# Shifted copies of two pairs of score tiles made by one VectorE instruction, in a planned attention and MLP kernel

## The chip, the core and the metric

The kernel runs on one core of one Trainium2 chip. The metric is the time on the device in microseconds, the median of the runs shown. Engines are named as in the profile: PE is TensorE (PEld its weight loads), DVE is VectorE, ACT is ScalarE, POOL is GpSimd, SP is SyncE, which issues the DMAs.

## What is computed

Two rounds of the same two layers, with the same weights each time, on x of 2048 tokens by 512 features in bfloat16:

```python
def _A_ref(x, wqkv, wo):            # H = 32 heads of Dh = 16
    q, k, v = ...                   # (x @ wqkv) split in heads
    p = _softmax(einsum("bhqd,bhkd->bhqk", q, k) * Dh ** -0.5)
    return heads_joined(einsum("bhqk,bhkd->bhqd", p, v)) @ wo

def _B_ref(x, w1, b1, w2, b2):      # F = 1376
    h = _gelu(einsum("bsd,df->bsf", _layernorm(x), w1) + b1)
    return einsum("bsf,fd->bsd", h, w2) + b2

x = x + _A_ref(_layernorm(x), A_wqkv, A_wo)
x = x + _B_ref(_layernorm(x), B_w1, B_b1, B_w2, B_b2)
# and both once more
```

The softmax over 2048 keys, for 2048 queries and 32 heads, twice, is the bulk: 268 million exponentials. In tiles of 128 keys by 512 queries that is 4096 tiles.

## The kernel before

**Tiles and stages.** The work is split in segments: a group of four heads (`hg`, eight of them) and a block of query tokens (512, in the last quarter of the second round 256, 128 and 128). For a segment, PE multiplies K and Q of one head and 128 keys into one bank of PSUM (`score`, L1512): a tile of 128 keys by 512 columns. Four heads sit in four row groups of PE. Then the tile is exponentiated in one of two ways.

- On ACT (L1497): PE fills two or three banks, banks 0 to 2 and 3 to 4 in turn, and one ACTIVATE makes `PT` of all of them (`flow_scores`).
- On DVE (`take_d`, `d_load`, `job_d`), for the key blocks in `DK` only: one TENSOR_SCALAR adds a constant to the scores and writes them as 16-bit integers into `dp` (L1598, one tile). The bits of such an integer, read as bfloat16, are nearly an exponential. Its error repeats along the exponent, so the kernel uses four copies, shifted by 0, 32, 64 and 96 and weighted in the values `vs`, to average it. Tiles go in batches of two (`DBATCH`), which fill one row of `dp` of 1024 elements. The first shift (L1629) makes row u+1 from row u. The second (L1634) makes rows v and v+1 from rows u and u+1.

PE then multiplies each copy with its values into one bank of sums (`try_pv`, L1705), four heads side by side in column groups. A tile of ACT's takes one such product, a tile of DVE's four. When a segment is done, DVE transposes the sums and divides (L1735, L1761, L1771), SP transposes the result by DMA (L1780), and the output product, the layer norm, both MLP products (L1846, L1907) and the GELU on ACT (L1898) follow, placed between the scores of later segments. Zero products (L1401, L1403, L1405) fill gaps of PE (`refill`).

**Buffers.** `dp` has 14 rows, handed out as pairs (even, odd) from a pool, oldest first; the pool's list grows as pairs are given up by other uses. In certain stages one more pair is lent by `OT`, a tensor of its own (`dpu`, `dpp` pick the right one). A pair goes back to the pool when the last product that reads it has been planned.

**What sets the order.** Nothing is ordered on the chip but by the engines' queues. A planner in Python (`Sched`) holds the tasks of all engines, each with a priority and an assumed duration; it picks the task that can start first, by the assumed times, and writes it into its engine's queue (`Prog.op`). A task counts as ready on DVE if its data is there within `LOOK` = 0.05 us of the time at which DVE comes free. What instructions wait for is worked out from reads and writes of named parts, such as ("dp", u, w). The string `Hint.ORDER` switches some of the planner's thresholds, one character for each four groups of scores; it moves work between ACT and DVE and reorders PE. The lines of the shifts, which the change wraps:

```python
yield Task("dve", prio(), [I(lambda e: e.tensor_scalar(out=self.dpu(u + 1)[:, 0:N], in0=self.dpu(u)[:, 0:N], ...)])   # L1629
self.d_ready(bt, 1, u + 1, u, range(n))
v = yield ("get", "dp", sg["i"])
yield Task("dve", prio(), [I(lambda e: e.tensor_scalar(out=self.dpp(v)[:, :, 0:N], in0=self.dpp(u)[:, :, 0:N], ...)])  # L1634
```

Their assumed durations are 0.150 + 0.2605e-3 N and 0.150 + 0.521e-3 N us, and DVE is taken to be free 0.08 us before an instruction ends.

Of the kernel before, what the change touches and what calls it, by code (L numbers as in the profile page):

```python
# [8 lines left out]
BF16 = mybir.dt.bfloat16  # L9
# [3 lines left out]
U16 = mybir.dt.uint16  # L13
ACTF = mybir.ActivationFunctionType
ALU = mybir.AluOpType
# [20 lines left out]
SHIFT = (0, 32, 64, 96)  # L36
# [5 lines left out]
class _Op:  # L42
    __slots__ = ("eng", "fn", "reads", "writes", "pos", "deps", "sig", "count", "waits", "dmaq", "t0", "t1", "spec", "spare")

    def __init__(self, eng, fn, reads, writes):
        self.eng = eng
        self.fn = fn
        self.reads = reads
        self.writes = writes
        self.pos = -1  # L50
        self.deps = []
        self.sig = False
        self.count = 0
        self.waits = []
        self.dmaq = None
        self.t0 = 0.0
        self.t1 = 0.0
# [196 lines left out]

class Task:

    __slots__ = ("eng", "ops", "prio", "cb", "seq")

    def __init__(self, eng, prio, ops):
        self.eng = eng  # L260
        self.prio = prio
        self.ops = ops
        self.cb = None
        self.seq = 0


def I(fn, reads=(), writes=(), dur=0.3, same_ok=(), lat=None):
    return (fn, tuple(reads), tuple(writes), tuple(same_ok), dur, lat)
# [9 lines left out]
class Sched:  # L278
# [45 lines left out]
    def _step(self, gen, prio, val):  # L324
        while True:
# [24 lines left out]
            if kind == "ready":  # L350
                r = self.P.ready(req[1], req[2], ()) - AHEAD
                if r <= self.now:
# [6 lines left out]
    def release(self, name, slot):  # L359
        p = self.pools[name]  # L360
        if slot in p.retired:
            key = p.retired.pop(slot)
            self.mark(key)
            return
        if p.waiters:
            _, _, cb = heapq.heappop(p.waiters)
            cb(slot)
        else:
            p.free.append(slot)

    def retire(self, name, slot, key):
        p = self.pools[name]
# [43 lines left out]
    def scores_due(self, f, lim):  # L416

        first = None
        for t in self.pend["pe"]:
            if t.prio == 0.0:  # L420
                r = self.task_ready(t)
                if r > lim and (first is None or r < first):
                    first = r
        if first is None or first - f > HOLD_REACH:
            return None
# [19 lines left out]
    def run(self):  # L445
        while True:
            pick = None
            for e in ENGINES:
                c = self.best(e)
                if c is not None and (pick is None or c[0] < pick[0]):  # L450
                    pick = c
            if self.timers and (pick is None or self.timers[0][0] <= pick[0]):
                t, _, cb = heapq.heappop(self.timers)
                self.now = max(self.now, t)
                cb()
                continue
            if pick is None:
                break
            t = pick[1]
            self.now = max(self.now, pick[0])  # L460
            if t.eng == "pe" and self.filler is not None:
                gap = pick[0] - self.P.drain
                if gap > FILL_GAP:
                    self.filler(gap)
            self.pend[t.eng].remove(t)
            for (fn, reads, writes, same_ok, dur, lat) in t.ops:
                self.P.op(t.eng, fn, reads, writes, same_ok, dur, lat)
            if t.cb is not None:
                t.cb()
            if t.eng == "dve" and self.after_dve is not None:  # L470
                self.after_dve()
        if self.live or self.kwait:
            raise RuntimeError("scheduler stuck: %d live, keys %s, pools %s" % (self.live, list(self.kwait)[:8], [(n, len(p.free), len(p.waiters)) for n, p in self.pools.items() if p.waiters]))


AHEAD = 0.3
HOLD_REACH = 1.0
HOLD_LEAD = 0.45
FILL_GAP = 0.2
# [13 lines left out]
DBATCH = 2  # L493
DFLY = 4
DBACK = 2.0
NDP = 14
# [19 lines left out]
NN2 = 2  # L516
NEED2 = 0
DOT = True


HELD = {(3, 0): (3, 1)}
# [2 lines left out]
class Hint:  # L524
    BASE = dict(D_IDLE=1.2, PV_LEAST=0.75, HOLD_LATE=0.4, PV_NEAR=0.7, LIN2=9, D_STEAL=0, POST=0)
    MODES = (dict(), dict(D_IDLE=0.8), dict(D_IDLE=1.7), dict(PV_LEAST=0.6), dict(PV_LEAST=0.9), dict(HOLD_LATE=0.2), dict(HOLD_LATE=0.6), dict(PV_NEAR=0.4), dict(LIN2=0.9), dict(D_STEAL=1.0), dict(POST=1), dict(POST=2))
    STEP = 4
    ORDER = '617843148821304222410024330100010322200010402005142300045935291731905421304450012300445404028299551400009505333207404304200030002302391015000030510104040320034300330030059090225910306350630422003320070322304130078057891b143300430303032703000430001459928b9001b338492908900532301308540020000009440105408040a010010a0211'

    def mode(self, k):  # L530
        self.__dict__.update(self.BASE)
# [2 lines left out]
    def at(self, step):  # L534
        self.mode(int(self.ORDER[step], 36) if step < len(self.ORDER) else 0)

# [5 lines left out]
class Builder:  # L542
# [45 lines left out]
    def alloc(self, es):  # L588
        nc = self.nc
        S, NT, NC, NFC = self.S, self.NT, self.NC, self.NFC  # L590
        t = lambda name, shape, dt: es.enter_context(nc.sbuf_tensor(name, shape, dt))
# [25 lines left out]
        self.qraw = t("qraw", [128, 2, 512], BF16)  # L617
        self.QT = t("QT", [128, 3, 512], BF16)
        self.PT = t("PT", [128, 23, 512], BF16)
        self.dp = t("dp", [128, NDP, 1024], U16)  # L620
        self.vs = t("vs", [128, 3, 3, len(DK), 68], BF16)
        self.OT = t("OT", [128, 8, 512], BF16)
        self.accT = t("accT", [128, 2, 512], F32)
        self.ob = t("ob", [128, 16, 8, 16], BF16)
        self.obl = t("obl", [128, 128], BF16)
# [81 lines left out]

    def otd(self, hg):

        return [("dp", NDP + (hg - 4) // 2, w) for w in (0, 1)] if DOT and hg >= 4 else []  # L710

    def dpu(self, u):

        return self.dp[:, u, :] if u < NDP else self.OT[:, 2 * (u - NDP) + 4:2 * (u - NDP) + 6, :].rearrange("p a n -> p (a n)").bitcast(U16)

    def dpp(self, u):

        return self.dp[:, u:u + 2, :] if u < NDP else self.OT[:, 4:8, :].rearrange("p a n -> p (a n)").bitcast(U16).rearrange("p (u n) -> p u n", u=2)

    def dres(self, s):  # L720

# [86 lines left out]
    def build_startup_late(self):  # L808
# [4 lines left out]
        def fills():  # L813
# [17 lines left out]
            S_.mark(("wld",))  # L831
            yield ("keys", [("retd", 1)] if DOT else [("oproj", 3, 0)])
            for hg in (6, 7):
# [744 lines left out]
    def d_solo(self):  # L1578
# [5 lines left out]
        if d is not None:  # L1584
            S_.submit(Task("pe", D_PRIO, self.score(d[0], d[1], d[2])), cb=lambda: self.d_load(d))

    def close_batch(self):
        bt = self.batch
        self.batch = None
        bt["closed"] = True  # L1590
        if bt["loaded"] == len(bt["tiles"]):
            self.S_.spawn(self.job_d(bt), 2.0)
# [30 lines left out]
    def job_d(self, bt):  # L1623

        S_ = self.S_
        u, n, sg = bt["unit"], len(bt["tiles"]), bt["tiles"][0][0]
        N = 512 * n
        prio = lambda: 0.15 if not self.left(sg) and sg is self.segs[self.acc_seg] else 0.5 if self.left(sg) < DURGE else 2.5
        yield Task("dve", prio(), [I(lambda e: e.tensor_scalar(out=self.dpu(u + 1)[:, 0:N], in0=self.dpu(u)[:, 0:N], scalar1=float(SHIFT[1]), scalar2=None, op0=ALU.add),  # L1629
                                     [("dp", u, w) for w in range(n)], [("dp", u + 1, w) for w in range(n)] + self.dres(u + 1), 0.150 + 0.2605e-3 * N, (), "fast")])  # L1630
        self.d_ready(bt, 1, u + 1, u, range(n))
        v = yield ("get", "dp", sg["i"])
        self.need2 -= 1
        yield Task("dve", prio(), [I(lambda e: e.tensor_scalar(out=self.dpp(v)[:, :, 0:N], in0=self.dpp(u)[:, :, 0:N], scalar1=float(SHIFT[2]), scalar2=None, op0=ALU.add),  # L1634
                                     [("dp", u + i, w) for i in (0, 1) for w in range(n)], [("dp", v + i, w) for i in (0, 1) for w in range(n)] + self.dres(v) + self.dres(v + 1), 0.150 + 0.521e-3 * N, (), "fast")])
        for i in (0, 1):
            self.d_ready(bt, 2 + i, v + i, v, range(n))
        self.flying -= 1
        self.use_done(("dp", u))
# [88 lines left out]
    def job_segend(self, sg):  # L1728
# [15 lines left out]
        if nparts == 2 and part == 0:  # L1744
            yield Task("dve", 1.2, [I(lambda e: e.tensor_copy(out=self.rowA[:, hg, :], in_=T[:, :, 17]), [RA], [("rowA", hg)], 0.25)])
            if L == 3:
                yield ("keys", [("oproj", 1, self.NC - 1)] + ([("retd", 0)] if DOT else []))
            yield Task("pool", 1.2, [I(lambda e: e.tensor_copy(out=M, in_=T[:, :, 0:16]), [RA], RO + [("sq", k, i) for k in (2, 3) for i in (0, 1)], 0.5), I(lambda e: e.tensor_copy(out=den, in_=T[:, :, 16]), [RA], [RD], 0.2)])
# [279 lines left out]
    def build(self):  # L2028
        S_ = self.S_
# [29 lines left out]
        S_.when([("qst", 1, tt) for tt in range(self.NT)], lambda: lend(1) if (1, 0) in HELD else None)  # L2059
        S_.when([("scl", 3, 1)] + [("qst", 3, tt) for tt in range(self.NT)], lambda: lend(3))  # L2060
        if DOT:
            S_.when([("ot", 1, 0, hg) for hg in range(8)], lambda: S_.release("dp", NDP))
            S_.when([("ot", 1, self.NC - 1, hg) for hg in range(8)], lambda: S_.retire("dp", NDP, ("retd", 0)))
            S_.when([("ot", 3, 0, hg) for hg in range(8)], lambda: S_.release("dp", NDP))
            S_.when([("ot", 3, len(self.units[3]) - 3, hg) for hg in range(8)], lambda: S_.retire("dp", NDP, ("retd", 1)))
        S_.when([("qt", 0)], lambda: S_.spawn(self.flow_scores(), 0.0))
        S_.filler = self.fill_pe
        S_.after_dve = self.d_solo
        self.P.spare = lambda: (tuple(range(6)) if self.wide and ("scores_done",) not in S_.done else ()) + ((MISCB,) if MISCB in S_.pools["mb"].free else ())
        for L in (1, 3):  # L2070
            for qc in range(len(self.units[L])):
# [58 lines left out]
```

## Time and profile before

| | |
|---|---|
| median of 3 runs | 1539.67 us (1539.26 to 1542.47) |
| the profiled execution | 1539.8 us, its span 1538.0 us |
| granted TensorE clock | 1.000 |
| exponentials on ACT (L1497) | 1260 instructions, busy 1427.3 us |
| tiles loaded by DVE (L1598) | 893 into dp and 78 into OT |
| first shifts (L1629) | 450 in dp and 39 in OT |
| second shifts (L1634) | 399, 51 and 39, by where they read and write |
| first exponential | at 21.2 us; last one ends at 1523.1 us |

The span runs from the first to the last instruction. In the rows of the groups stand line, engine, operation, output and input with their shapes (partitions by elements) and the count, then busy time in us and the mean duration in ns, then the engine's idle time before these instructions and what ended it. A row of the waits has who waited, for whom, the sum in us, how often, and the longest. A row of the timeline has the start and the length in us. Busy time counts overlapping instructions of one engine once; two instructions that follow each other overlap in the records, so the time that a queue spends on one is better read from start to start.

### The profile page before, as it was taken

The numbers are of one execution on the slowest core, as the hardware profiler recorded it, in microseconds if no ns is written. First come the engines' busy times: TensorE is split into PE (matmuls) and PEld (weight loads), VectorE is DVE, ScalarE is ACT, GpSimd is POOL, SyncE is SP. The second block draws the span as 40 slices with busy tenths as digits, with TensorE's granted clock in tenths as the row PEclk, the third lists the DMA queues.
The fourth block names the chain that finished last, engine by engine and source line by source line (L and its number), as shares of the span: only waits on it lengthen the run. The fifth ranks groups of instructions, "written<-read, shape, count | busy, mean of one in ns | idle before, by whom it ended". The sixth has DMA issues, their size and how long they took to land.

```text
span 1538.0 us, 41184 instructions
## 1 busy us (share of the span) xinstructions
PE 1485.6 (97%) x17604; PEld 489.9 (32%) x17604; DVE 1449.5 (94%) x2835; ACT 1508.2 (98%) x1350; POOL 333.9 (22%) x570
## 2 busy tenths in 40 slices
PE   8999999999999999999999999999999999999998
PEld 3222322222222222222222223222322222444565
DVE  8799999999999999999999899999999989999796
ACT  8999999999999999999999999999999999999997
POOL 3586422002120021202222228320002000020120
PEclk9999999999999999999999999999999999999999
DMA  6663102213321222213932333310011010210221
GB/s 166 116 150 87 35 26 40 57 26 79 84 42 52 49 56 75 62 33 99 149 52 67 60 77 72 58 26 21 22 33 39 11 29 24 45 41 25 72 68 31
DMA packets 212488, 90.56 MB, mean 59 GB/s; under 512 B 182251, under 2 KB 207184, under 8 KB 212304
## 3 DMA queue, kind: packets, MB, share of 16 engines
q1 hardware_dynamic: 212304, 87.92, 26.0%
q8 instruction: 138, 2.26, 0.6%
q14 instruction: 46, 0.38, 0.1%
HBM read 36.81 MB, written 19.48 MB: 37 GB/s over the span
## 4 chain that ended last, share of the span: by engine, by line
ACT 52%; PE 22%; DVE 21%; issue 2%; POOL 1%; SPq 1%; DMA 1%; POOLq 0%; DVEq 0%
ACT PT L1497 49%; DVE dp L1598 7%; PE ps L1512 7%; PE ps L1705 6%; DVE dp L1634 3%; PE ps L1907 3%; PE ps L1846 3%; DVE dp L1629 2%; ACT h L1898 2%; PE ps L992 2%; DVE st L909 1%; DVE accT L1735 1%; SPq L1780 1%; DMA OT<-ob 1%; DVE OT L1598 1%
## 5 line engine op out<-in xcount | busy, mean ns | idle before, releaser
L1497 ACT ACTIVATE PT<-ps 128x1536 bf16<-128x1536 f32 (+1 forms) x1260 | 1427.3, 1303 | 17.2 <-PE ps L1512 15.1
L1598 DVE TENSOR_SCALAR dp<-ps 128x512 uint16<-128x512 f32 x893 | 595.8, 681 | 33.4 <-PE ps L1512 30.8
L1512 PE MATMUL ps<-QT,KT 32*128 32x512 bf16 (+2 forms) x5120 | 599.5, 339 | 28.2 <-ACT PT L1497 10.9
L1705 PE MATMUL ps<-PT,V 128*17 128x512 bf16 (+2 forms) x3908 | 482.1, 338 | 0.0
L1705 PE MATMUL ps<-dp,vs 128*17 128x512 bf16 (+2 forms) x3318 | 433.5, 337 | 0.7 <-DVE dp L1634 0.4
L1512 PEld LDWEIGHTS ps<-QT,KT 32*128 32x128 bf16 x5120 | 172.5, 91 | 546.5 <-ACT PT L1497 307.2
L1634 DVE TENSOR_SCALAR dp<-dp 128x2048 uint16<-128x2048 uint16 (+1 forms) x399 | 277.2, 701 | 2.9 <-PE ps L1705 0.2
L1238 POOL TENSOR_SCALAR QT<-qraw,scl,qbias 128x512 bf16<-128x512 bf16 (+2 forms) x91 | 75.7, 832 | 766.0 <-PE ps L1512 753.6
L1705 PE MATMUL ps<-dp,V 128*17 128x512 bf16 (+2 forms) x1128 | 202.9, 337 | 1.5 <-DVE accT L1735 1.4
L1629 DVE TENSOR_SCALAR dp<-dp 128x1024 uint16<-128x1024 uint16 (+1 forms) x450 | 187.4, 428 | 2.3
L1405 PE MATMUL ps<-zw 128*32 128x448 bf16 (+25 forms) x1466 | 163.8, 324 | 0.4 <-DVE dp L1598 0.4
L1705 PEld LDWEIGHTS ps<-PT,V 128*17 128x17 bf16 x3908 | 124.7, 89 | 91.6 <-issue 75.0
L1705 PEld LDWEIGHTS ps<-dp,vs 128*17 128x17 bf16 x3318 | 117.9, 89 | 101.0 <-issue 74.8
L1403 PE MATMUL ps<-zw 32*128 32x444 bf16 (+2 forms) x387 | 120.5, 332 | 0.0
L1846 PE MATMUL ps<-yT,wf 128*128 128x512 bf16 (+5 forms) x440 | 103.7, 341 | 3.5 <-DVE dp L1629 1.5
L992 PE MATMUL ps<-wqkv,xnT 128*128 128x512 bf16 x336 | 92.1, 382 | 2.4 <-DVE dp L1005 0.9
L1401 PE MATMUL ps<-zw 128*128 128x448 bf16 (+16 forms) x371 | 90.1, 339 | 3.4 <-DVE onec L785 2.1
L1705 PE MATMUL ps<-OT,vs 128*17 128x512 bf16 (+2 forms) x318 | 78.0, 356 | 0.0
L1263 POOL TENSOR_SCALAR vs<-V 128x340 bf16<-128x340 bf16 (+2 forms) x72 | 62.7, 872 | 25.5 <-PE ps L1705 22.0
L1735 DVE STREAM_TRANSPOSE accT<-ps 128x512 f32<-128x512 f32 (+2 forms) x96 | 59.2, 617 | 7.0 <-PE ps L1705 7.0
L1405 PEld LDWEIGHTS ps<-zw 128*32 128x32 bf16 x1466 | 58.3, 95 | 19.6 <-DVE dp L1598 2.5
L1705 PEld LDWEIGHTS ps<-dp,V 128*17 128x17 bf16 x1128 | 50.8, 88 | 36.1 <-issue 18.3
(207 smaller groups left out, 1173.3 us busy)
## 6 DMA issues: line engine op xcount, KB each, us to landing
vs<-vs_scr SPq DMA_DIRECT2D x64, 255.0 KB, 2.7
wf<-in_B_w_dram SPq DMA_DIRECT2D x90, 128.0 KB, 2.5
q_scr<-qk SPq DMA_DIRECT2D x20, 256.0 KB, 2.0
k_scr<-qk SPq DMA_DIRECT2D x12, 256.0 KB, 2.0
out_dram<-xres SPq DMA_DIRECT2D x16, 128.0 KB, 1.7
vs_scr<-vs SPq DMA_DIRECT2D x8, 255.0 KB, 3.1
xres<-in_A_x_dram SPq DMA_DIRECT2D x7, 256.0 KB, 5.3
v_scr<-vst SPq DMA_DIRECT2D x12, 136.0 KB, 1.8
```

Of the source, the lines that this page charges most:

```text
L992: yield Task("pe", prio if c0 == 0 else min(prio, HINT.LIN2), [I(lambda e, c=c: e.matmul(self.ps[:, b, :], lhsT=xnT[:, c, :], rhs=self.wqk ...
L1238: yield Task(eng, 0.4, [I(lambda e: e.tensor_scalar(out=self.QT[:, q, 0:W], in0=src, scalar1=self.scl[:, k, hg:hg + 1], scalar2=self.qbias ...
L1401: fn = lambda e: e.matmul(self.ps[:, b, 0:w], lhsT=self.zw[:, 0:128], rhs=self.zw[:, 0:w], start=st, stop=st, skip_group_check=True)
L1403: fn = lambda e: e.matmul(self.ps[:, b, 0:w], lhsT=self.zw[32 * p:32 * p + 32, 0:128], rhs=self.zw[32 * p:32 * p + 32, 0:w], start=st, sto ...
L1405: fn = lambda e: e.matmul(self.ps[32 * p:32 * p + 32, b, 0:w], lhsT=self.zw[:, 0:32], rhs=self.zw[:, 0:w], start=st, stop=st, skip_group_c ...
L1497: S_.submit(Task("act", 1e-5 * gi, [I(lambda e, pt=pt, n=n, b0=b0: e.activation(out=self.PT[:, pt:pt + n, :], in_=self.ps[:, b0:b0 + n, :] ...
L1512: return [I(lambda e, kb=kb, i=i: e.matmul(self.ps[:, b, i * W:(i + 1) * W], lhsT=self.KT[32 * hp:32 * hp + 32, hg, kb * 128:(kb + 1) * 12 ...
L1598: self.S_.submit(Task("dve", 0.0, [I(lambda e: e.tensor_scalar(out=self.dpu(u)[:, w * 512:(w + 1) * 512], in0=self.ps[:, b, :], scalar1=BI ...
L1629: yield Task("dve", prio(), [I(lambda e: e.tensor_scalar(out=self.dpu(u + 1)[:, 0:N], in0=self.dpu(u)[:, 0:N], scalar1=float(SHIFT[1]), sc ...
L1634: yield Task("dve", prio(), [I(lambda e: e.tensor_scalar(out=self.dpp(v)[:, :, 0:N], in0=self.dpp(u)[:, :, 0:N], scalar1=float(SHIFT[2]), ...
L1705: ops.append((nth[j, sh] + 0.1 * i, I(lambda e, hp=hp, v=v, ap=ap[:, i * W:(i + 1) * W], first=first and i == 0, W=W: e.matmul(self.ps[32 ...
L1846: yield Task("pe", self.soft(pr if c0 == 0 else min(pr, HINT.LIN2)) if y0 == 0 else pr, [I(lambda e, c=c: e.matmul(self.ps[0:M, b, 0:W], l ...
```

## The change

A shift of a full batch (two tiles) carries a `mate`: its kind (1 or 2) and its rows. When the planner picks such a task, it looks for another of the same kind on DVE that is ready by then and whose rows lie in the same order, and emits one instruction for both, over two rows with the distance of the two batches as step. The joined instruction reads and writes what both did and waits for both; what follows either is released after it. It is planned 0.15 us shorter than both together.

So that two batches can be one access pattern, the pair of rows lent by `OT` moves behind the 14 rows of `dp` into one tensor (`bits`, 18 rows, of which the last four are `OT`; `LENT` is 16). The pool of pairs is sorted after each release, so that the lowest pair goes out first. And `Hint.ORDER` is a new string.

```diff
+            if name == "dp":
+                p.free.sort()
...
+            both = None
+            if t.mate is not None:
+                lim = max(pick[0], self.P.free["dve"]) + self.LOOK["dve"]
+                both = next((o for o in self.pend["dve"] if o.mate is not None and o.mate[0] == t.mate[0] and (o.mate[1] < t.mate[1]) == (o.mate[2] < t.mate[2]) and self.task_ready(o) <= lim), None)
+            if both is not None:
+                self.pend["dve"].remove(both)
+                (fn, reads, writes, same_ok, dur, lat), more = t.ops[0], both.ops[0]
+                x, y = sorted((t.mate[1:], both.mate[1:]))
+                self.P.op("dve", self.join(t.mate[0], x, y), reads + more[1], writes + more[2], same_ok, dur + more[4] - SHIFT_FIXED, lat)
+                for o in sorted((t, both), key=lambda o: o.mate[1:]):
+                    o.cb()
+            else:
...
+SHIFT_FIXED = 0.15
...
+LENT = NDP + 2
...
-        self.dp = t("dp", [128, NDP, 1024], U16)
+        self.bits = t("dp", [128, NDP + 4, 1024], U16)
+        self.dp = self.bits[:, 0:NDP, :]
...
-        self.OT = t("OT", [128, 8, 512], BF16)
+        self.OT = self.bits[:, NDP:NDP + 4, :].bitcast(BF16).rearrange("p u (a n) -> p (u a) n", n=512)
...
+    def both(self, a, b, o=None):
+
+        if o is not None:
+            return self.bits[:, a + o:b + o + 1:b - a, :]
+        return self.bits[:, :, :].rearrange("p (u a) n -> p u (a n)", a=2)[:, a // 2:b // 2 + 1:(b - a) // 2, :]
...
+    def d_join(self, kind, x, y):
+
+        if kind == 1:
+            return lambda e: e.tensor_scalar(out=self.both(x[0], y[0], 1), in0=self.both(x[0], y[0], 0), scalar1=float(SHIFT[1]), scalar2=None, op0=ALU.add)
+        return lambda e: e.tensor_scalar(out=self.both(x[1], y[1]), in0=self.both(x[0], y[0]), scalar1=float(SHIFT[2]), scalar2=None, op0=ALU.add)
...
+        if n == DBATCH:
+            t.mate = (1, u, u)
+        yield t
...
+        if n == DBATCH:
+            t.mate = (2, u, v)
+        yield t
```

`ORDER` is changed from its 17th character on; its 315 or so characters are not shown.

## The prediction

> **What bounds the kernel now.** I read the busy table of the page first, then the groups by shape, then the waits, then the timeline of VectorE (DVE) and of ScalarE (ACT).
>
> ```profile
> PE 1485.6 (97%) x17604; PEld 489.9 (32%) x17604; DVE 1449.5 (94%) x2835; ACT 1508.2 (98%) x1350; POOL 333.9 (22%) x570
> ...
> ACT 52%; PE 22%; DVE 21%; issue 2%; POOL 1%; SPq 1%; DMA 1%; POOLq 0%; DVEq 0%
> ```
>
> Three engines are nearly full. PE's 97% holds filler (the zero matmuls from zw at L1401, L1403 and L1405), so its real load is less. ACT has 29.8 us without work (1538.0 - 1508.2), and about half of the chain is ACT's exponentials. The groups by shape say what ACT and DVE do:
>
> ```profile
> L1497 ACT ACTIVATE PT<-ps 128x1536 bf16<-128x1536 f32 x606 | 923.5, 1524 | 14.0 <-PE ps L1512 12.1
> L1497 ACT ACTIVATE PT<-ps 128x1024 bf16<-128x1024 f32 x653 | 711.9, 1099 | 3.2 <-PE ps L1512 3.0
> ...
> L1598 DVE TENSOR_SCALAR dp<-ps 128x512 uint16<-128x512 f32 x893 | 595.8, 681 | 33.4 <-PE ps L1512 30.8
> L1634 DVE TENSOR_SCALAR dp<-dp 128x2048 uint16<-128x2048 uint16 x393 | 274.3, 704 | 2.9 <-PE ps L1705 0.2
> L1629 DVE TENSOR_SCALAR dp<-dp 128x1024 uint16<-128x1024 uint16 x443 | 185.6, 430 | 2.3
> L1598 DVE TENSOR_SCALAR OT<-ps 128x512 uint16<-128x512 f32 x78 | 52.5, 680 | 0.8 <-PE ps L1512 0.6
> ```
>
> ACT takes 606 x 3 + 653 x 2 score tiles, and one more in a single-tile instruction outside these rows: 3125. DVE takes 893 + 78 = 971. Together they are 4096, which is all of them. So the two engines share one fixed heap of tiles, and what DVE gains in time is worth something only as far as tiles move from ACT to DVE. Idle before the exponentials is 17.2 us (14.0 + 3.2); ACT is the engine whose work sets the end. The waits show how far the others reach it:
>
> ```profile
> PEld ps L1512 <- ACT PT L1497: 307.2, 774, 1.0
> ...
> PEld ps L1512 <- DVE dp L1598: 68.6, 176, 1.1
> ...
> ACT PT L1497 <- PE ps L1512: 15.1, 45, 1.7
> ...
> PE ps L1512 <- DVE dp L1598: 6.7, 23, 0.8
> ...
> PEld ps L1512 <- DVE OT L1598: 3.8, 11, 0.5
> ```
>
> Scores mostly wait for ACT to free a bank, as is right where ACT is the bound. They wait 79.1 us for DVE's copies (68.6 + 6.7 + 3.8), but ACT waits only 15.1 us for scores: at most 0.19 of the former arrives at ACT.
>
> **The joining, per instruction.** The durations of L1629 and L1634 have medians of 419 and 685 ns, so 1024 more elements cost 266 ns and each instruction has 153 ns besides. The timeline of DVE says that this isn't what the queue loses:
>
> ```profile
> 1509.58 0.42 DVE L1629 TENSOR_SCALAR dp<-dp 128x1024 uint16<-128x1024 uint16 x1
> 1509.91 0.68 DVE L1598 TENSOR_SCALAR dp<-ps 128x512 uint16<-128x512 f32 x1
> 1510.51 0.68 DVE L1634 TENSOR_SCALAR dp<-dp 128x2048 uint16<-128x2048 uint16 x1
> 1511.11 0.34 DVE L1875 TENSOR_SCALAR h<-ps,b1c 128x128 bf16<-128x128 f32 x1
> ...
> 809.41 0.42 DVE L1634 TENSOR_SCALAR dp<-dp 128x1024 uint16<-128x1024 uint16 x1
> 809.74 0.42 DVE L1629 TENSOR_SCALAR dp<-dp 128x1024 uint16<-128x1024 uint16 x1
> ```
>
> From start to start, L1629 takes 0.33 us and L1634 takes 0.60 (the medians over the trace, where the next one doesn't wait for it). Two first shifts take 0.66, one of double size 0.60; two second shifts 1.20, one of double size 0.60 + 2 x 0.27 = 1.14. Each joining frees 0.06 us. The Trainium skill ("VectorE: DVE Perf Modes", The DRAIN you can't avoid) says that the next instruction does not start until the pipe is empty; by that the whole 153 ns would be freed, 188 x 0.153 = 28.8 us. The same page's cycle table (The TRN2 errata) has a fixed 58 cycles at 0.96 GHz, 60 ns. The trace decides for the second, since starts overlap the end before by some 0.08 us. And the errata's advice, to tile at 512 elements or more so that the fixed cost is spread, speaks against a large gain: 1024 elements are beyond that already.
>
> Does the two-row form keep its rate? The row at 809.41 is two rows of 512 (the only shape in which L1634 has 1024): 0.42 us and 0.33 to the next start, like 1024 in one row. I take the same slope. Were it to run at half the rate, a joined first shift would cost 0.53 more and a second 1.06: 97 x 0.53 + 91 x 1.06 = 148 us. Nothing in the trace points there.
>
> **Part by part**, with counts from the built program, without running it.
> - DVE: 97 first shifts and 91 second shifts stand for two each, so 188 instructions go and 188 x 0.06 = 11.3 us are freed. Eight more tiles are loaded (979): 8 x 0.60, and four more pairs of shifts, 4 x (0.33 + 0.60), together 8.5 us. Net: 2.8 us less, lying beside ACT. Shifts that directly follow what they wait for (0.45 instead of 0.33 us from start to start) stay as frequent: first to second 94 before, 87 after; load to first 74 and 75.
> - ACT: 605 instructions of three tiles and 651 of two: 3117. One of three, two of two and the one of a single tile are gone. 36 in a row take 40.39 us from 1376.36, so a pair of both sizes takes 2.244; the sizes differ by 1524 - 1099 = 425 ns. That makes 1.335, 0.91 and, one step down, 0.485. Gone: 1.335 + 1.82 + 0.485 = 3.6 us. This is on the path. Table loads and GELUs are the same in number.
> - PE: eight tiles need 24 more value products, at four side by side in about 0.22 us: 1.3 us, and filler gives way. Nothing on the path; without that cover 1.3 us.
> - The waits added: a joined shift waits for both its pairs, and the planner only joins what it holds ready within 0.05 us. Its price is in DVE's queue: what stands behind it starts later, by 0.27 or 0.54 us, than behind one half. In the built order that is 67 loads behind a joined first shift and 58 behind a joined second. PE's next score waits for those loads, and ACT waits for that. The plan carries the longer time, so I take nothing and keep the price for the rival below. Below nothing: the second half of a pair is ready 0.06 us sooner.
> - The sorted pool hands out the lowest free buffer, often one just given back. 67 second shifts waited for a value product on PE before, 128 do now. The nearest row is the one such stall in the trace, 0.2 us (L1634's releaser). 61 x 0.2 = 12 us on DVE if all stall, x 0.19 = 2.3 us at ACT. I take nothing: 66 of the 67 found the product done.
> - POOL (574) and SP (545) have as many instructions as before, and no DMA is added. The last four transposes of ob keep their place ahead of the last two stores; their landing (1524.66) and the last VectorE transpose (1524.67) ended together, so the tail may give or take 1 us.
> - The new string reorders PE throughout. Its effect on ACT's 17.2 us of waiting can't be read from an order without times: between -6 and +9 us (the rivals), and I take 0, the nearest row being the present one.
>
> The sum: ACT 1508.2 - 3.6 = 1504.6, plus 29.8 idle, is a span of 1534.4; the 1.8 us around it (1539.8 for the profiled run, span 1538.0) give 1536.2. The median shown lies 0.1 below that run: **1536.1 us**.
>
> **Rivals.**
> - ACT waits less. If the shorter DVE work takes a quarter to two fifths of the 15.1 us away, 3.8 to 6, the time is 1530 to 1532. For it: 79 us of score waits for DVE. Against: DVE ends up only 2.8 us lighter.
> - The saving is eaten: ACT waits 2 to 6.7 us more, 1538 to 1542.8. For it: buffer waits nearly double.
> - Slower: the loads queued behind joined shifts. 67 x 0.27 + 58 x 0.54 = 49 us of later loads, x 0.19 = 9.3 us more waiting on ACT: 1545.4. It decides once ACT's waits grow by over 6.7 us (3.6 + 3.1). Against it: no DVE instruction of 1.14 us is new to PE, since two separate shifts in a row (46 and 69 such neighbours in the order before) held loads as long.
> - The two-row form is slow: beyond 1600. That the joining doesn't happen is excluded by the counts.
>
> **How the numbers follow.** A measurement of this kernel can tell about 0.2%, 3.1 us: faster is below 1536.6, slower above 1542.8. Forecast, waits within 2 us of now (1534 to 1538): 0.46, of which 0.32 below 1536.6. Less waiting: 0.26. Eaten: 0.10. Loads late: 0.16. Slow form: 0.02. Faster 0.58, same 0.24, slower 0.18. The range, 1530.5 to 1543.5, leaves out the slow form, most of the late loads and a little below.
>
> **What would show it.** 3117 tiles at 1.335 and 0.91 us, ACT's busy time near 1504.6; joined shifts near 0.69 us and 1.22 us (0.60 and 1.14 to the next start); DVE busy some 3 us less. Right if ACT's idle before exponentials stays at 15 to 19 us. Wrong if it grows past 24, with score waits for the load line above 79 us by tens; or if joined shifts take 1.2 and 2.3 us.

## The result and the profile after

Over 14 runs each, the changed kernel takes 1536.93 us (median) and the kernel before 1539.78: the ratio is 0.9976, with a 95% interval of 0.9966 to 0.9987. That is 3.7 us faster by the ratio (0.0024 x 1539.8) and 2.85 by the medians, just about what a measurement of this kernel can tell; the forecast was 1536.1. The profiled execution took 1537.7 us, its span 1535.9.

The busy table and the chain of the changed kernel:

```profile
PE 1486.8 (97%) x17654; PEld 491.3 (32%) x17654; DVE 1442.2 (94%) x2661; ACT 1502.5 (98%) x1346; POOL 343.0 (22%) x570
...
ACT 44%; PE 27%; DVE 24%; issue 3%; POOL 2%; DMA 0%; DVEq 0%; POOLq 0%
```

ACT is busy for 5.7 us less and DVE for 7.3 less, but the span is only 2.1 shorter: ACT's time without work has grown from 29.8 to 33.4 us. The chain runs less through ACT (44% after 52%) and more through PE and DVE. The groups by shape, first ACT's exponentials, then DVE:

```profile
L1521 ACT ACTIVATE PT<-ps 128x1536 bf16<-128x1536 f32 x605 | 924.6, 1528 | 14.6 <-PE ps L1536 13.2
L1521 ACT ACTIVATE PT<-ps 128x1024 bf16<-128x1024 f32 x651 | 712.5, 1105 | 5.9 <-PE ps L1536 5.7
...
L1628 DVE TENSOR_SCALAR dp<-ps 128x512 uint16<-128x512 f32 x979 | 648.8, 679 | 33.7 <-PE ps L1536 30.4
L1667 DVE TENSOR_SCALAR dp<-dp 128x2048 uint16<-128x2048 uint16 x305 | 212.2, 699 | 4.9 <-PE ps L1741 1.8
L1659 DVE TENSOR_SCALAR dp<-dp 128x1024 uint16<-128x1024 uint16 x293 | 124.7, 429 | 2.6
L1615 DVE TENSOR_SCALAR dp<-dp 128x4096 uint16<-128x4096 uint16 x91 | 111.0, 1225 | 0.6 <-PE ps L1741 0.4
L1614 DVE TENSOR_SCALAR dp<-dp 128x2048 uint16<-128x2048 uint16 x97 | 67.8, 700 | 0.0
```

L1614 and L1615 are the joined shifts, 97 and 91, at 700 and 1225 ns. Idle before the exponentials is 20.5 us here (14.6 + 5.9), 17.2 before. DVE's second shifts now wait for PE, which means for buffers: 1.8 us at L1667 and 0.4 at L1615, where it was 0.2. And the waits:

```profile
PEld ps L1536 <- DVE dp L1628: 78.1, 218, 1.0
...
ACT PT L1521 <- PE ps L1536: 18.8, 48, 2.5
```

Scores wait a little longer for DVE's loads: 82.9 us with the 4.8 of PE's own row, not shown, against 79.1 before. ACT waits longer for scores (18.8, 15.1 before).

Busy time is no pure count of work. The kernel of the first experiment below has the same 1256 exponentials, and ACT is busy 4.3 us longer in it (1506.8) while it waits more often. So the 5.7 us need not all be tiles.

So the numbers look like the forecast. The experiments ask whether its reasons hold: that ScalarE's work sets the end one for one, and that VectorE's queue lies beside it. Ratios are to the kernel before, timed beside each.

### The profile page after: what moved, and what is told of

Same layout as the page of the kernel before. It is cut to its first block, busy times and chain, and to the rows that moved or that the text cites. A ratio compares the mean times of both kernels' runs of the same rounds, so it can differ in the third digit from the quotient of the medians.

```text
span 1535.9 us, 41170 instructions
## 1 busy us (share of the span) xinstructions
PE 1486.8 (97%) x17654; PEld 491.3 (32%) x17654; DVE 1442.2 (94%) x2661; ACT 1502.5 (98%) x1346; POOL 343.0 (22%) x570
## 4 chain that ended last, share of the span: by engine, by line
ACT 44%; PE 27%; DVE 24%; issue 3%; POOL 2%; DMA 0%; DVEq 0%; POOLq 0%
ACT PT L1521 41%; DVE dp L1628 10%; PE ps L1536 9%; PE ps L1741 8%; PE ps L1943 3%; DVE dp L1667 3%; PE ps L1882 2%; PE ps L1016 2%; ACT h L1934 2%; DVE dp L1615 2%; DVE dp L1659 1%; PE ps L1425 1%; DVE accT L1771 1%; DVE st L933 1%; DVE dp L1614 1%
## 5 line engine op out<-in xcount | busy, mean ns | idle before, releaser
L1521 ACT ACTIVATE PT<-ps 128x1536 bf16<-128x1536 f32 (+1 forms) x1256 | 1422.0, 1309 | 20.6 <-PE ps L1536 18.8
L1628 DVE TENSOR_SCALAR dp<-ps 128x512 uint16<-128x512 f32 x979 | 648.8, 679 | 33.7 <-PE ps L1536 30.4
L1536 PE MATMUL ps<-QT,KT 32*128 32x512 bf16 (+2 forms) x5120 | 602.6, 340 | 23.9 <-ACT PT L1521 7.5
L1741 PE MATMUL ps<-PT,V 128*17 128x512 bf16 (+2 forms) x3899 | 491.1, 338 | 0.6 <-issue 0.5
L1741 PE MATMUL ps<-dp,vs 128*17 128x512 bf16 (+2 forms) x3663 | 460.8, 339 | 2.7 <-issue 1.8
L1536 PEld LDWEIGHTS ps<-QT,KT 32*128 32x128 bf16 x5120 | 174.1, 91 | 543.6 <-ACT PT L1521 297.6
L1741 PE MATMUL ps<-dp,V 128*17 128x512 bf16 (+2 forms) x1221 | 232.3, 340 | 1.6 <-DVE accT L1771 1.2
L1667 DVE TENSOR_SCALAR dp<-dp 128x2048 uint16<-128x2048 uint16 x310 | 214.3, 694 | 4.9 <-PE ps L1741 1.8
L1741 PEld LDWEIGHTS ps<-dp,vs 128*17 128x17 bf16 x3663 | 124.1, 89 | 114.1 <-issue 84.8
L1741 PEld LDWEIGHTS ps<-PT,V 128*17 128x17 bf16 x3899 | 126.9, 89 | 94.2 <-issue 75.1
L1429 PE MATMUL ps<-zw 128*32 128x448 bf16 (+23 forms) x1514 | 147.1, 322 | 0.1
L1659 DVE TENSOR_SCALAR dp<-dp 128x1024 uint16<-128x1024 uint16 (+1 forms) x298 | 126.1, 426 | 2.6
L1427 PE MATMUL ps<-zw 32*128 32x444 bf16 (+7 forms) x386 | 119.5, 332 | 0.0
L1615 DVE TENSOR_SCALAR dp<-dp 128x4096 uint16<-128x4096 uint16 x91 | 111.0, 1225 | 0.6 <-PE ps L1741 0.4
L1425 PE MATMUL ps<-zw 128*128 128x448 bf16 (+14 forms) x347 | 87.4, 338 | 4.4 <-DVE onec L809 2.1
L1741 PEld LDWEIGHTS ps<-dp,V 128*17 128x17 bf16 x1221 | 58.2, 89 | 34.6 <-issue 19.4
L1614 DVE TENSOR_SCALAR dp<-dp 128x2048 uint16<-128x2048 uint16 x97 | 67.8, 700 | 0.0
```

Of the source, the lines that this page charges most:

```text
L1425: fn = lambda e: e.matmul(self.ps[:, b, 0:w], lhsT=self.zw[:, 0:128], rhs=self.zw[:, 0:w], start=st, stop=st, skip_group_check=True)
L1427: fn = lambda e: e.matmul(self.ps[:, b, 0:w], lhsT=self.zw[32 * p:32 * p + 32, 0:128], rhs=self.zw[32 * p:32 * p + 32, 0:w], start=st, sto ...
L1429: fn = lambda e: e.matmul(self.ps[32 * p:32 * p + 32, b, 0:w], lhsT=self.zw[:, 0:32], rhs=self.zw[:, 0:w], start=st, stop=st, skip_group_c ...
L1521: S_.submit(Task("act", 1e-5 * gi, [I(lambda e, pt=pt, n=n, b0=b0: e.activation(out=self.PT[:, pt:pt + n, :], in_=self.ps[:, b0:b0 + n, :] ...
L1536: return [I(lambda e, kb=kb, i=i: e.matmul(self.ps[:, b, i * W:(i + 1) * W], lhsT=self.KT[32 * hp:32 * hp + 32, hg, kb * 128:(kb + 1) * 12 ...
L1615: return lambda e: e.tensor_scalar(out=self.both(x[1], y[1]), in0=self.both(x[0], y[0]), scalar1=float(SHIFT[2]), scalar2=None, op0=ALU.add)
```

## The experiments

### Joined shifts taken apart, in place

```diff
-                self.P.op("dve", self.join(t.mate[0], x, y), reads + more[1], ...)
+                first, second = (fn, more[0]) if x == t.mate[1:] else (more[0], fn)
+                self.P.op("dve", lambda e, first=first, second=second: (first(e), second(e))[1], reads + more[1], ...)
```

> The order of the changed kernel, but each of the 188 joined shifts is issued as the two single shifts in the same place, with the same waits and one signal after the second. VectorE has 188 x 0.06 = 11.3 us more in its queue and nothing else is moved. If ScalarE sets the end and VectorE reaches it by at most 0.19 of its delay, the time is 0 to 2.1 us above the changed kernel (1536.9), so 1537 to 1539. If VectorE is as much a bound as ScalarE, most of the 11.3 us arrive: 1545 to 1548. If the long joined instructions themselves hold up loads, the time falls below 1536.9.

Measured: 1548.74 us, ratio 1.0039 (1.0027 to 1.0052). Against the changed kernel that is 1.0039 / 0.9976 = 1.0063, or 9.7 us more; from the ends of both intervals, 6 to 13. The timelines of DVE show the same place in both kernels, first the changed one, then the one taken apart:

```profile
153.74 0.68 DVE L1614 TENSOR_SCALAR dp<-dp 128x2048 uint16<-128x2048 uint16 x1
154.34 0.68 DVE L1628 TENSOR_SCALAR dp<-ps 128x512 uint16<-128x512 f32 x1
154.94 1.21 DVE L1615 TENSOR_SCALAR dp<-dp 128x4096 uint16<-128x4096 uint16 x1
156.08 0.68 DVE L1628 TENSOR_SCALAR dp<-ps 128x512 uint16<-128x512 f32 x1
```

```profile
153.31 0.75 DVE L1660 TENSOR_SCALAR dp<-dp 128x1024 uint16<-128x1024 uint16 x2
153.98 0.68 DVE L1629 TENSOR_SCALAR dp<-ps 128x512 uint16<-128x512 f32 x1
154.58 1.28 DVE L1668 TENSOR_SCALAR dp<-dp 128x2048 uint16<-128x2048 uint16 x2
155.78 0.68 DVE L1629 TENSOR_SCALAR dp<-ps 128x512 uint16<-128x512 f32 x1
```

Read the starts: a joined first shift holds the queue for 0.60 us (153.74 to 154.34), two single ones for 0.67; a joined second for 1.14, two single ones for 1.20. This is the 0.06 to 0.07 us of the forecast. DVE is busy for 14.8 us more in all. The busy table, the chain and the waits of the kernel taken apart (131 of its PE records are missing, so PE reads low):

```profile
PE 1469.3 (95%) x17523; PEld 491.6 (32%) x17654; DVE 1457.0 (94%) x2849; ACT 1506.8 (98%) x1346; POOL 336.4 (22%) x570
...
DVE 47%; PE 24%; ACT 23%; issue 4%; POOL 2%; DMA 0%; DVEq 0%; POOLq 0%
```

```profile
PEld ps L1537 <- DVE dp L1629: 92.2, 246, 1.0
...
ACT PT L1522 <- PE ps L1537: 21.5, 59, 2.5
```

Half of the chain now lies on DVE. My theory gave at most 2.1 us, and most of what was added arrived: a delay on VectorE does not stay beside the path in this order. With this order and these tiles the joining is worth 9.7 us; without it the changed order would be slower than the kernel before.

### The same with two signals, and with loads ahead of the second halves

Here the halves are separate instructions with their own waits; in the second kernel, 125 second halves go behind the load that follows them.

```diff
+        if move:
+            ...                      # second half k == 1 at i, next DVE instruction at j a load from PSUM
+            specs[i:j + 1] = specs[i + 1:j + 1] + [(s, None)]
```

> As the split in place, but each half has its own waits and its own signal, so that value products of the first half need not wait for the second. If readiness of the first half matters, faster than the split with one signal, by up to 2 us; by my theory products have slack and it is the same within 1 us: 1537 to 1539.

> As the split with two signals, but in the 125 places where a load from PSUM stands directly behind a joined shift, the second half goes behind that load. These loads come 0.27 or 0.54 us earlier, 49 us in all. If loads late behind joined shifts cost ScalarE time (my rival: 0.19 of 49 us), up to 9 us faster than the split with two signals, and faster than the changed kernel; if not, the same as the split within 1.5 us.

Measured: 1549.35 us, 1.0046 (1.0034 to 1.0058), for two signals: the same as with one. With the loads first 1559.64 us, 1.0112 (1.0099 to 1.0125): slower by 1.0112 / 1.0046 = 1.0066, or 10 us (6 to 14 from the ends of both intervals). The waits for DVE, of the kernel with two signals and of the one with loads first:

```profile
PEld ps L1539 <- DVE dp L1631: 93.6, 244, 1.0
...
PEld ps L1744 <- DVE dp L1670: 9.4, 31, 0.6
...
PEld ps L1744 <- DVE dp L1662: 6.5, 21, 0.7
```

```profile
PEld ps L1539 <- DVE dp L1631: 81.9, 222, 1.0
...
PEld ps L1744 <- DVE dp L1670: 19.0, 41, 1.2
PEld ps L1744 <- DVE dp L1662: 14.8, 28, 1.1
...
PE ps L1744 <- DVE dp L1670: 6.3, 15, 0.9
```

L1539 is the score product, L1744 the value product. With loads first, scores wait less for loads (81.9 us, 93.6 with two signals), as meant, but value products wait 33.8 us for shifts instead of 15.9, and PE's queue stands behind them. So nothing is to be gained by letting the loads go first: in this order the shifts are needed just as soon. What the loads' later place behind a joined shift costs by itself is not shown, since the same edit makes the second halves late.

### ScalarE's work cut, nothing moved

```diff
-I(lambda e, pt=pt, n=n, b0=b0: e.activation(out=self.PT[:, pt:pt + n, :], in_=self.ps[:, b0:b0 + n, :], ...
+I(lambda e, pt=pt, m=2 if less else n, b0=b0: e.activation(out=self.PT[:, pt:pt + m, :], in_=self.ps[:, b0:b0 + m, :], ...
```

> The kernel before, with nothing moved, but in 8 of the three-tile exponentials, spread over the run, only two of the three tiles are exponentiated (the exponentials of 8 tiles of 4096 are left out). ScalarE has 8 x 0.425 = 3.4 us less, the other engines the same. If ScalarE's work goes to the end one for one, 1539.8 - 3.4 = 1536.4. If the other engines hold the pace, 1538 to 1540: then the gain of the change came from elsewhere.

> The kernel before, but in 30 of the three-tile exponentials only two tiles are exponentiated (30 of 4096 tiles are left out on ScalarE). ScalarE has 30 x 0.425 = 12.8 us less. One for one: 1527. If the others hold the pace, the gain stops early: 1531 to 1537. Likely in between, 1530, as VectorE and TensorE have only 5 to 6% of slack.

Measured: 1542.81 us, 1.0002 (0.9990 to 1.0013), with 8 tiles less, and 1540.36 us, 0.9991 (0.9982 to 1.0000), with 30 less. The exponentials' groups of the two, from their pages:

```profile
L1500 ACT ACTIVATE PT<-ps 128x1536 bf16<-128x1536 f32 (+1 forms) x1260 | 1424.4, 1293 | 22.1 <-PE ps L1515 19.9
```

```profile
L1500 ACT ACTIVATE PT<-ps 128x1536 bf16<-128x1536 f32 (+1 forms) x1260 | 1418.3, 1268 | 27.1 <-PE ps L1515 23.7
```

Before, this row has 1427.3 us busy and 17.2 idle. Cut by 2.9 and 9.0 us, ACT waits 4.9 and 9.9 us more before its exponentials. Part of this is not the cut's: the kernel before, timed beside these two, takes 1543.3 and 1541.6 us, and 1539.8 where its 17.2 us were profiled. The same number of tiles by which the change relieves ACT, taken away alone, is worth 0 (at most 1.5 us, by the interval). The forecast's main step is refuted for a fixed order.

### VectorE's work cut, then TensorE's filler, then all

```diff
+        H = N // 2 if n == 2 and self.n2nd > 60 and self.n2nd % 10 == 4 else N      # VectorE
-        ... out=self.dpp(v)[:, :, 0:N], in0=self.dpp(u)[:, :, 0:N]
+        ... out=self.dpp(v)[:, :, 0:H], in0=self.dpp(u)[:, :, 0:H]
+        c = int(0.8 * w)                                                            # filler
-        ... self.ps[:, b, 0:w], ... rhs=self.zw[:, 0:w]
+        ... self.ps[:, b, 0:c], ... rhs=self.zw[:, 0:c]
```

> The kernel before, with nothing moved, but 42 of the second shifts, spread over the run, shift only half of each row (the shifted copies of the other halves are left out). VectorE has 42 x 0.27 = 11.3 us less, as much as the split in place had more. If VectorE alone sets the pace, 0.86 of it arrives, as with the split: 10 us less than before, ratio 0.9937. If an engine cut alone gains nothing, because the fixed order ties the three queues together, 0 to 3 us: 0.998 to 1.000, as with the cuts of ScalarE's work.

> Both cuts at once in the kernel before: 30 tiles left out of ScalarE's exponentials (12.8 us) and 42 second shifts halved on VectorE (11.3 us). If ScalarE and VectorE are bounds side by side, most of the smaller cut arrives: 8 to 11 us, ratio 0.993 to 0.995. If TensorE's queue, filler included, is the floor, no more than the cuts one by one: 0.997 to 0.999. If VectorE alone is the bound, the same as its cut alone.

> The kernel before with every filler product of TensorE in its place but of 0.8 of its columns (they compute nothing that is used). TensorE has 0.2 x 133.9 = 27 us less if all counted as full-array work. If TensorE's queue, full with filler, sets the pace, several us less than before (0.995 to 0.998), unless the granted clock falls; if filler only lies in waits, the same as before within 1.5 us (1.000).

> All three cuts at once in the kernel before: 30 tiles out of ScalarE's exponentials, 42 second shifts halved, filler at 0.8 of its columns. If the three queues are tied, this gains more than the sum of the cuts one by one: 10 to 12 us, ratio 0.992 to 0.9935. If filler costs nothing, the same as the two cuts of ScalarE and VectorE together.

| cut from the kernel before | median | ratio |
|---|---|---|
| 42 second shifts halved (DVE) | 1540.96 us | 0.9993 (0.9984 to 1.0002) |
| and 30 tiles (ACT) | 1539.03 us | 0.9985 (0.9976 to 0.9994) |
| filler at 0.8 of its columns (PE) | 1541.67 us | 1.0005 (0.9997 to 1.0014) |
| all three | 1538.46 us | 0.9982 (0.9973 to 0.9991) |

The busy table with the filler cut alone, then the busy table and the exponentials with all three cuts:

```profile
PE 1473.6 (96%) x17604; PEld 492.0 (32%) x17604; DVE 1449.1 (94%) x2835; ACT 1507.7 (98%) x1350; POOL 334.1 (22%) x570
```

```profile
PE 1473.4 (96%) x17604; PEld 492.1 (32%) x17604; DVE 1440.4 (94%) x2835; ACT 1498.4 (98%) x1350; POOL 333.2 (22%) x570
...
L1501 ACT ACTIVATE PT<-ps 128x1536 bf16<-128x1536 f32 (+1 forms) x1260 | 1417.5, 1277 | 25.0 <-PE ps L1516 22.4
```

With all three, PE has 12.2 us less, DVE 9.1, ACT 9.8, and the time falls by 0.0018 x 1541.8 = 2.8 us. The filler cut alone lowered PE's busy time by 12.0 us and gained nothing. None of the three gives back what is taken off it, as a floor would. TensorE's own products were not shortened in any run, so whether they set the pace in places stays open: of the 22% of the chain that lie on PE before, the page gives 21% to them (scores 7%, value products 6%, the products of L1907, L1846 and L992 8%).

### The old string

```diff
-    ORDER = '61784314882130420550310702472320900004020704304234...'
+    ORDER = '61784314882130422241002433010001032220001040200514...'
```

The first has joining and the sorted pool, the second joining and the pool oldest first (without `p.free.sort()`), the third the sorted pool and no shift with a `mate`.

> Joining and sorted pool with the string of the kernel before. By the built order it has 152 joined shifts, VectorE takes 967 tiles (971 before, 979 after) and ScalarE 608 instructions of three tiles, 652 of two and one of one. By ScalarE's work: 2 x 1.335 - 0.91 = 1.8 us more than before, so 1541.6, give or take the waits. If the joining itself brings the gain through a shorter VectorE queue, 1536 to 1538.

> Joining with the old string and the pool oldest first, 137 joined shifts. VectorE takes 964 tiles, ScalarE 612 instructions of three tiles, 648 of two, one of one: 6 x 1.335 - 5 x 0.91 = 3.5 us more than before, 1543.3 by its work. Beside the same with the pool sorted (1541.6 by its work) it shows what the sorting does.

> The changed kernel's buffers and sorted pool, the old string, no shift joined. VectorE takes 961 tiles, ScalarE 613 instructions of three tiles, 648 of two, one of one: 7 x 1.335 - 5 x 0.91 = 4.8 us more on ScalarE than before, so 1544.6 by its work. If a plan that the string was not chosen for has more waits as well, several us above that; if the sorting is harmless and tiles do not set the time, 1540.

Measured: 1583.31 us, 1.0262 (1.0244 to 1.0281); 1583.99 us, 1.0271 (1.0258 to 1.0285); 1594.07 us, 1.0316 (1.0296 to 1.0337). The tile counts gave 1541.6, 1543.3 and 1544.6, so they missed by some 40 us. Sorting makes no difference that these runs can tell (1.0262 and 1.0271). The first is 8 us faster than the third (1.0262 / 1.0316 = 0.9948), but the two are different plans, with 967 and 961 tiles on DVE, so this isn't the joining alone. The exponentials of the first kernel, and one of the places where ACT waits in it, ACT's timeline and PE's below it:

```profile
L1521 ACT ACTIVATE PT<-ps 128x1536 bf16<-128x1536 f32 (+2 forms) x1261 | 1438.3, 1265 | 50.3 <-PE ps L1536 45.0
```

```profile
702.13 2.37 ACT L1521 ACTIVATE PT<-ps 128x1024 bf16<-128x1024 f32 x2 [3.17 <-PE ps L1536]
```

```profile
698.68 1.46 PE L1943 MATMUL ps<-wf,h 128*128 128x512 bf16 x6
699.98 0.38 PE L1943 MATMUL ps<-wf,g 128*128 128x512 bf16 x1
...
701.38 0.39 PE L1741 MATMUL ps<-dp,vs 128*17 128x512 bf16 x2
701.70 0.61 PE L1536 MATMUL ps<-QT,KT 32*128 32x512 bf16 x6
```

ACT waits 3.17 us, while PE's fixed queue has MLP products (L1943) and value products (L1741) ahead of the scores (L1536). In this kernel ACT's idle before exponentials is 50.3 us, 17.2 before; the plan also holds more filler, 158.6 us of full-array work by the columns in the built program, 129.3 in the changed kernel and 133.9 in the one before. More gaps were planned, and more waiting came.

The plan says so itself, for the planner writes a time to each task, from its assumed durations. Planned again from the kernels, the last task ends at 1531.8 us in the kernel before and 2.9 us earlier in the changed one (measured 3.7 by the ratio). In the three with the old string it ends 44, 49 and 49 us later (measured 40, 42 and 49), and 8 and 22 us later with the halves apart and with the loads first (measured 7 and 17).

The fourth corner, the new string without joining, was not run: such a plan runs out of pairs of `dp` and never comes to its end. A string fitted anew to the kernel before was not run either.

## Why the prediction was right, and where its reasons were not

**Right: the price of a joining and the counts.** 0.60 us and 1.14 from start to start and 0.70 and 1.22 us long, for two rows apart as for one; 188 joined, 979 and 3117 tiles. (The eight tiles more on DVE are five full batches more and two of one tile fewer, not four more pairs, which changes the sum by some 0.1 us.) The fixed cost in the cycle table of the Trainium skill ("VectorE: DVE Perf Modes", The TRN2 errata), 58 cycles or 60 ns, agrees with the 0.06 to 0.07 us that a joining frees here. The 28.8 us set against it were no rival: the section The DRAIN you can't avoid of the same page goes on that a next instruction starts earlier where nothing holds it, and so it is here, with starts 0.60 us apart for a length of 0.68.

**Failed: "This is on the path", of ScalarE's 3.6 us.** Measured, ACT's busy time fell by more (5.7 us), yet the span by 2.1 and the idle before exponentials rose by 3.3, to 20.5 us: above the 15 to 19 that the prediction named as its sign of being right, and below the 24 of being wrong. Alone, such a cut gave nothing with 8 tiles and 1.4 us of 12.8 with 30. That 1539.8 - 3.6 lands near the measured time is luck: ACT's busy time was missed by 2.1 us one way and its time without work by 3.6 the other way (29.8 to 33.4).

**Failed: "Net: 2.8 us less, lying beside ACT", and the share of 0.19.** 11.3 us by the sum (14.8 in busy time) put back on VectorE cost 9.7: a share of 0.86 or 0.66. By the ends of the intervals the cost is 6 to 13 us, so 0.19 is excluded (2.1 us). The share was taken from two sums of waits in an order that ran as planned; it said nothing about work that comes on top. Whether "I take nothing" was right for the joined shift's place in the queue stays open: to let the loads pass cost 10 us, since the shifts are due as early as the loads.

**Failed: that the string's effect "can't be read from an order without times", and so is 0.** Against the kernel before, ACT's waiting rose by 3.3 us, within the -6 to +9 that the prediction allowed. But the times are there, in the plan, and its end would have given -2.9 us for the change. The forecast also left out how much hangs on the string: with the old one the changed planner's kernel is 2.6% slower, and even without joining, with the buffers and the sorted pool alone, 3.2%. By these runs the old string suits the old planner alone.

**What the runs put in place of it.** Both parts are needed: without joining the new order is at 1.0039, without the new string joining is at 1.0262, and together they are at 0.9976. In the new plan both ACT and DVE have less to do by its counts. In a given order a delay of 0.06 us at 188 places passed on, and relief of 0.27 or 0.43 us at 42 or 30 places was mostly lost. The reading that fits is that every queue stands next to another that is almost as late.

**Open.** That relief is lost because the neighbouring queue has only a little slack at each place is argued from the waits that grew (17.2 to 27.1 us on ACT) and not shown place by place. Even all three cuts together gave 2.8 us; they lie at different places, and no run put them at the same ones. The delay was put into the new order and the cuts were taken from the old one, at other places and of another size. By an estimate from the planner's assumed times, with each order kept, that isn't what makes the difference: 0.06 us more at 188 shifts picked at random costs 6 to 8 us in the old order and 5 to 6 in the new, and 0.06 us less there gains under 1 us in both. (For the cuts above it gives 0 to 1.5 us.) No run shows it. Whether a string fitted anew would have gained as much without joining is open too, so the 3.7 us can't be put down to the joining alone, nor divided between ScalarE's and VectorE's relief.

## What to carry to other kernels

When the order is fixed ahead and several engines are 94 to 98% busy, test each with a delay and with a cut, in the same order, since the two can disagree: the one tells what must not grow, the other what is worth shrinking. Don't price a moved piece of work by the sum of the busiest engine alone. When the order comes from a planner, read its planned end as well as its counts. And when a cheaper instruction goes in, lay the order anew before judging it: here the same change is 2.6% slower or 0.24% faster by the order alone.

## What the runs show of the hardware

- As the prediction took it, a joined shift over two rows some distance apart has the same rate as elements that lie together: 700 ns for 2 x 1024 (L1614), 699 for 2048 in neighbouring rows (L1667).
- With a fifth of the filler columns gone, TensorE's granted clock stayed at 1.000 in the profiled execution (0.996 to 1.000 over all runs; 0.997 to 1.000 in the kernel before, beside it); that much filler was not needed for it in this kernel.
